# Reordering a few matmuls in the weight-loading chunk, and issuing two late stores from GpSimd

## The chip, the cores and the metric

The kernel runs on one core of one Trainium2 chip. The metric is the device time of one execution in microseconds (us), taken from several executions. The profile of one execution gives a trace of every instruction. The span in a trace, from the first to the last instruction, is 1.9 to 2.2 us shorter than the time of the same run, so traces can be compared by their spans.

The engines are PE (matmuls), ACT (ScalarE), DVE (VectorE), POOL (GpSimd) and SP (the sync engine, which mostly issues DMAs).

## The reference

Linear attention over 8 batches and 8 heads (sequence 576, head size 64), and then one MLP over all 4608 rows:

```python
q_s = softmax(q, axis=-1)          # written out with exp, max and sum
k_s = softmax(k, axis=2)
kv  = einsum('bhsd,bhse->bhde', k_s, v)
x   = einsum('bhsd,bhde->bhse', q_s, kv)      # -> 4608 x 512
h   = x @ w_in                     # 512 -> 2048
g   = h * (1.0 / (1.0 + exp(-beta * h)))
return g @ w_out                   # 2048 -> 512, float32
```

## The kernel before

The rows are worked off in 9 chunks of 512 rows: the first 512 rows of each batch, and one last chunk with the 64-row tails of all eight. A chunk has 16 MLP units. Unit `u` is a first product `h_u` (`mm_a`, 4 matmuls of 128x512), a tanh `th_u` on ACT, a combination `g_u` on DVE, and a second product into `acc_0` to `acc_3` (`mm_b`, 4 matmuls). The second product runs two units behind the first (`LAG = 2`). The order of each engine's instructions is fixed by hand, by the order in which the program names them; in the timelines below the engines' work comes in that order.

Chunk 0 is special. It runs while the weights are still being loaded: `w_in` comes in four blocks of 512 columns and `w_out` in four blocks of rows, each cast from float32 to bfloat16, most of them by GpSimd, in two halves. Units 12 to 15 need block 3 of `w_in`. Beside it the attention part of batch 1 is prepared: exponentials of q on ACT (`q_exp`), their sums and the multiplication by the inverse sums on DVE (`q_sum`, `q_mul`, the tile is `eq_485`), transposes on PE (`q_pet`, tiles `tp_0` to `tp_3`) with copies to `qsT`, eight exponentials of k on ACT (`kz_exp`, tile `ek`), and then the products `kv_0` and `kv_1`, from which chunk 1 gets its input.

```python
    tail_zero(0)
    pool_cast(("out", 1), ("in", 2), ("out", 2))
    tail_zero(1)
    pool_cast(("in", 3), ("out", 3))          # GpSimd's own order

    for u in range(4, NJ):
        mm_a(0, u)
        mm_b(0, u - LAG)
        if u in (9, 10):
            q_exp(1, u - 9)
        if u in (9, 11):
            q_sum(1, (u - 9) // 2)
        if u in (10, 12):
            q_mul(1, (u - 10) // 2)
        if u in (11, 13):
            for j in (u - 11, u - 10):
                q_pet(1, j, nc.scalar if u == 11 else nc.vector)
        if u >= 12:
            kz_exp(1, u - 12)
        if u == 14:
            vz_cast(1, 0, nc.vector, m=2)
    mm_b(0, NJ - 2)
    # ... kv_mm(1, 0), kv_mm(1, 1), last mm_b, x_mm(1, 0..3), then chunk 1
```

So PE's order around unit 12 is: `h_11`, second product of unit 9, transposes `tp_0` and `tp_1`, `h_12`, second product of unit 10.

The second part concerns the end of the kernel, the last stores of the last chunk:

```python
    def store(c, st):
        ...
        if c == B:
            lo, hi = ((0, 2), (0, 2), (2, 3), (3, 4))[st]
            ...
            evac(eng, o[:, st, :], acc[st][:])          # ACT for even st, DVE for odd
            if st == hi - 1:
                for e in range(2):
                    (nc.scalar if st == 2 or (st == 3 and e) else nc.sync).dma_start(...)
```

The two stores of `o_2` (128 KB each) and one half of `o_3` are issued by the scalar engine, the rest by sync.

The softmax here doesn't subtract the row's maximum and nothing guards it: scores larger than these inputs give would overflow.

Of the kernel before, what the change touches and what calls it, by code (L numbers as in the profile page):

```python
# [17 lines left out]
def kernel(  # L18
# [23 lines left out]
    NW = 2  # L42
    D1 = D + 1
    LAG = 2
    NCH = B + 1

    const = ctx.enter_context(tc.tile_pool(name="const", bufs=1))
    stage = ctx.enter_context(tc.tile_pool(name="stage", bufs=1))
# [203 lines left out]
    def kv_mm(b, jj, n=2, tag="att"):  # L252
        t = ps.tile([P, n, 2 * D1], F32, tag=tag, bufs=2 if tag == "att" else 1, name=f"kv{b}_{jj}")
        att_of[b, jj] = t
        for jl in range(n):
            j = n * jj + jl
            if b < NW:
                for i in range(RW):
                    nc.tensor.matmul(
                        t[:, jl, 0:D1],  # L260
                        ek[b][:, j, i, :],
                        va[b][:, j, i, :],
                        start=(i == 0),
                        stop=(i == RW - 1),
                    )
                continue
            for i in range(R):
                nc.tensor.matmul(
                    t[:, jl, :],
                    ek[b][:, i, 2 * j : 2 * j + 2, :].rearrange("p h d -> p (h d)"),  # L270
                    va[b][:, i, 2 * j : 2 * j + 2, :].rearrange("p h d -> p (h d)"),
                    start=(i == 0),
                    stop=False,
                )
            nc.tensor.matmul(
                t[:, jl, :],
                ekt[(b // 2) % 2][:, ds(j * P, P)],
                vt[(b // 2) % 2][:, b % 2, 2 * j : 2 * j + 2, :].rearrange("p h d -> p (h d)"),
                start=False,
                stop=True,  # L280
            )

    def kv_norm(b, jj, n=2):
        t = att_of.pop((b, jj))
        rk = work.tile([P, n, 1], F32, tag="rk", bufs=2, name=f"rk{b}_{jj}")
        nc.vector.reciprocal(rk[:], t[:, :, D : D + 1])
        for e in range(2):
            r = slice(e * D, (e + 1) * D)
            dst = kvp[r, b, n * jj : n * jj + n, e * D : (e + 1) * D]
            src = t[r, :, 0:D] if b < NW else t[r, :, e * D1 : e * D1 + D]  # L290
            nc.vector.tensor_tensor(dst, src, rk[r].to_broadcast((D, n, D)), ALU.mult)  # L291

    def x_mm(c, j, eng, tag="att"):
# [62 lines left out]
    def store(c, st):  # L356
        acc = acc_of[c]
        eng = nc.scalar if st % 2 == 0 else nc.vector
        if c == B:
            lo, hi = ((0, 2), (0, 2), (2, 3), (3, 4))[st]  # L360
            if st == lo:
                o_of[c] = stage.tile([P, R, DM], F32, tag="wo", bufs=4, name=f"o{c}_{lo}")
            o = o_of[c]
            evac(eng, o[:, st, :], acc[st][:])
            if st == hi - 1:
                for e in range(2):
                    (nc.scalar if st == 2 or (st == 3 and e) else nc.sync).dma_start(
                        out_t[:, MAIN:S, :].rearrange("(i e) t f -> e t i f", e=2)[e, :, lo:hi, :],
                        o[e * TAIL : (e + 1) * TAIL, lo:hi, :],
                    )  # L370
            return
        if st == 0:
            o_of[c] = stage.tile([P, R, DM], F32, tag="wo", bufs=4, name=f"o{c}")
        o = o_of[c]
        evac(eng, o[:, st, :], acc[st][:])
        if st % 2 == 1:
            ov = out[c * S : c * S + MAIN, :].rearrange("(p i) f -> p i f", i=R)
            nc.sync.dma_start(ov[:, st - 1 : st + 1, :], o[:, st - 1 : st + 1, :])
# [41 lines left out]
    ek_buf(1, nc.gpsimd)  # L420
    v_buf(1)

    def load_next(nb):
        if nb < B:
            load_q(nb)
            load_kv(k_st, k, nb, "k_st")
            load_kv(v_st, v, nb, "v_st")
        elif nb == B:
            load_qtail()

    def finish_b(c, j):
        mm_b(c, j)
        if j == NJ - 1:
            for st in range(R):
                store(c, st)
# [47 lines left out]
    w_cast("in", 1, 1, nc.vector)  # L483
    mm_b(0, 0)
    mm_b(0, 1)
    def pool_cast(*what):
        for kind, blk in what:
            for half in range(2):
                w_cast(kind, blk, half, nc.gpsimd)
# [10 lines left out]
    pool_cast(("in", 3), ("out", 3))  # L500

    for u in range(4, NJ):
        mm_a(0, u)
        mm_b(0, u - LAG)
        if u in (9, 10):
            q_exp(1, u - 9)
        if u in (9, 11):
            q_sum(1, (u - 9) // 2)
        if u in (10, 12):
            q_mul(1, (u - 10) // 2)  # L510
        if u in (11, 13):
            for j in (u - 11, u - 10):
                q_pet(1, j, nc.scalar if u == 11 else nc.vector)
        if u >= 12:
# [3 lines that stand above are left out]
# [17 lines left out]
    mm_b(1, 0)  # L535
    mm_b(1, 1)

    def side(c, u):
        b = c + 1
        if b > B:  # L540
            return
        tail = b == B
        o = 2 if c == 1 else 0
        if u in (2 + o, 3 + o):
            q_exp(b, u - 2 - o)
            q_sum(b, u - 2 - o)
        if u in (4 + o, 5 + o):
            q_mul(b, u - 4 - o)
            if not tail:
                k_exp(b, u - 4 - o)  # L550
        if u == 4 + o and not tail:
            v_buf(b)
            v_cast(b, nc.gpsimd)
            vtail_cast(b, nc.gpsimd)
        if u == 6 + o:
            if not tail:
                ktail_exp(b)
            q_xbar(b)
        if u in (8 + o, 10 + o) and not tail:
            kv_mm(b, (u - 8 - o) // 2)  # L560
            kv_norm(b, (u - 8 - o) // 2)
        if 11 <= u < 15:
            j = u - 11
            x_mm(b, j, nc.scalar if j % 2 == 0 else nc.vector)
        if u == 9:
            load_next(c + 2)

    for u in range(4):
        side(1, u)
    for c in range(1, NCH):  # L570
        for j in range(4 if c == 1 else 0, NJ - 1 if c == B else NJ):
            lead = c > 1 and j == 3
            if not lead:
                mm_a(c, j)
            if c > 1 and j == 2:
                mm_a(c, 3)
            if (c, j) == (B, NJ - 2):
                pass
            elif j >= LAG:
                mm_b(c, j - LAG)  # L580
            else:
                finish_b(c - 1, NJ + j - LAG)
            side(c, j)
    mm_a(B, NJ - 1, tag="att")
    last = [(0, j) for j in range(NJ - 4, NJ - 1)] + [(1, j) for j in range(NJ - 4, NJ - 1)]
    last += [(0, NJ - 1), (1, NJ - 1)] + [(st, j) for st in (2, 3) for j in range(NJ - 4, NJ)]
    for st, j in last:
        mm_b(B, j, [st])
        if j == NJ - 1:
            store(B, st)  # L590
# [1 line left out]
_INS = ['q', 'k', 'v', 'moe_w_in', 'moe_w_out', 'moe_beta']  # L592
_OUTS = [((4608, 512), 'float32')]
# [25 lines left out]
```

## Time and profile before

| what | value |
|---|---|
| time, median of 3 runs | 293.87 us (293.31 to 294.41) |
| profiled run: time, span, granted clock | 294.54 us, 292.4 us, 0.996 |
| PE busy | 279.5 us, 96% |
| PE idle before `acc_0` of unit 2 | 0.86 us |
| PE idle before `tp_0` | 1.59 us |
| end of the last copy (`o_3`) to the end of the span | 5.36 us |

From the page of the kernel before: its span, its part 1 (busy time of each engine with its share of the span and instruction count) and the engines' shares of part 4, the chain of waits that ended last.

```profile
span 292.4 us, 3879 instructions
PE 279.5 (96%) x1447; PEld 131.0 (45%) x1475; DVE 184.2 (63%) x299; ACT 163.9 (56%) x238; POOL 42.0 (14%) x55
PE 85%; DMA 6%; DVE 2%; ACT 1%; issue 1%; SPq 1%; another core or an unknown queue 1%; POOL 0%; ACTq 0%
```

PE is the bottleneck. From about 49 us to the last products it has no gaps worth naming, so only its gaps in chunk 0 and the tail after its last matmul can be won.

The timeline of the kernel before, in chunk 0. The columns are start in us, duration in us, engine, source line, operation, output and inputs, their shapes, the count; in square brackets the idle time of the engine just before, and what ended it.

```profile
22.15 1.37 POOL L140 CAST w_out_b<-w_out_100 128x1024 bf16<-128x1024 f32 x1 [4.28 <-DMA w_out_100<-in_moe_w_out_dram]
23.57 0.38 PE L344 MATMUL acc_0_377<-w_out_b,g_2_365 128*128 128x512 bf16 x1 [0.86 <-POOL w_out_b L140]
...
36.01 3.01 POOL L140 CAST w_in_b<-w_in_114 128x1024 bf16<-128x1024 f32 x2 [2.12 <-DMA w_in_114<-in_moe_w_in_dram]
36.04 2.09 DVE L226 TENSOR_TENSOR eq_485<-eq_485,rq_487 128x1024 bf16<-128x1024 bf16 x1
38.27 0.39 PE L245 MATMUL tp_0_521<-identity,eq_485 128*128 128x128 bf16 x4 [1.59 <-DVE eq_485 L226]
38.71 1.03 PE L316 MATMUL h_12_533<-xT_80,w_in_b 128*128 128x512 bf16 x4
39.78 0.69 ACT L326 ACTIVATE th_12_538<-h_12_533,beta_t 128x512 bf16<-128x512 f32 x1
```

Two gaps of PE: 0.86 us at 23.57, behind a GpSimd cast of `w_out` block 0, and 1.59 us at 38.27, behind the DVE multiply `eq_485`. GpSimd's cast of `w_in` block 3 (two halves, 36.01 to 39.02) starts before that multiply, when its DMA (landed at 35.89) has come in.

The timeline of the kernel before, at the end (SPq and ACTq are DMA issues on the sync and the scalar engine), and the DMA view of the same stores (the last column is the median time from issue to landing, in us).

```profile
286.06 1.31 ACTq L367 DMA_DIRECT2D out_dram<-o_2_2904  x2
286.31 0.69 DVE L140 COPY o_3_2912<-acc_3_2730 128x512 f32<-128x512 f32 x1 [1.03 <-PE acc_3_2730 L344]
287.03 0.95 SPq L367 DMA_DIRECT2D out_dram<-o_3_2912  x1
287.47 1.76 ACTq L367 DMA_DIRECT2D out_dram<-o_3_2912  x1
```

```profile
out_dram<-o_2_2904 ACTq DMA_DIRECT2D x2, 128.0 KB, 3.8
out_dram<-o_3_2912 SPq DMA_DIRECT2D x1, 128.0 KB, 4.2
out_dram<-o_3_2912 ACTq DMA_DIRECT2D x1, 128.0 KB, 4.0
```

The copy of `o_3` ends at 287.00. Sync issues its half at once, but the scalar queue is still issuing the stores of `o_2` and gets to its half only at 287.47.

### The profile page before, as it was taken

The page shows a single profiled execution, that of the slowest core. Times are in us where ns is not written, and L with a number is a line of the kernel's source. Part 1 is how long each engine was busy: PE and PEld are TensorE (multiplying, and loading weights), DVE is VectorE, ACT ScalarE, POOL GpSimd, SP SyncE. Part 2 cuts the span into 40 slices and gives each one's busy share as a digit, 9 for nine tenths or more (in the row PEclk, how much of TensorE's full clock was granted, in tenths as well). Part 3 has the DMA queues.
Part 4 walks back from the last instruction along what each step waited for, and adds up shares of the span by engine and source line. Part 5 has one row for each costly group of instructions (what it writes and reads, how often), then busy time and mean ns, then how long its engine had stood idle before and what let it go on. Part 6 is the DMA issues. An engine that isn't in the chain of part 4 may idle for free.

```text
span 292.4 us, 3879 instructions
## 1 busy us (share of the span) xinstructions
PE 279.5 (96%) x1447; PEld 131.0 (45%) x1475; DVE 184.2 (63%) x299; ACT 163.9 (56%) x238; POOL 42.0 (14%) x55
## 2 busy tenths in 40 slices
PE   8898979999999999999999999999999999999991
PEld 3443435445444444454445444544454444544440
DVE  7853696695578557855695469456954694563441
ACT  4863666684486448734773567346825654453340
POOL 4539670300030021002100110003000000000000
PEclk9999999999999999999999999999999999999998
DMA  7999999708932963297319821981293023012005
GB/s 243 378 385 371 377 385 311 248 2 233 296 152 62 315 162 123 62 326 177 123 40 302 223 90 54 303 234 64 84 165 52 32 115 72 0 58 87 0 0 144
DMA packets 55971, 50.06 MB, mean 171 GB/s; under 512 B 26241, under 2 KB 47761, under 8 KB 55953
## 3 DMA queue, kind: packets, MB, share of 16 engines
q1 hardware_dynamic: 55712, 49.43, 55.8%
q10 hardware_dynamic: 240, 0.39, 0.5%
q8 instruction: 11, 0.18, 0.3%
q14 instruction: 8, 0.06, 0.1%
HBM read 36.71 MB, written 9.44 MB: 158 GB/s over the span
## 4 chain that ended last, share of the span: by engine, by line
PE 85%; DMA 6%; DVE 2%; ACT 1%; issue 1%; SPq 1%; another core or an unknown queue 1%; POOL 0%; ACTq 0%
DMA w_out_100<-in_moe_w_out_dram 4%; DMA v_st_91<-in_v_dram 2%; PE acc_3_724 L344 1%; PE acc_2_2458 L344 1%; PE acc_0_2456 L344 1%; PE acc_3_2459 L344 1%; PE acc_1_2167 L344 1%; PE acc_1_1300 L344 1%; PE acc_1_1589 L344 1%; PE acc_1_2728 L344 1%; PE acc_1_1011 L344 1%; PE acc_1_722 L344 1%; PE acc_1_1878 L344 1%; PE acc_2_1879 L344 1%; PE acc_2_1590 L344 1%; PE acc_0_721 L344 1%
## 5 line engine op out<-in xcount | busy, mean ns | idle before, releaser
L316 PEld LDWEIGHTS <-w_in_b 128*128 128x128 bf16 x576 | 55.3, 98 | 65.5 <-issue 2.7
L386 PEld LDWEIGHTS <-kvp 128*128 128x128 bf16 x34 | 3.7, 117 | 6.2 <-issue 3.6
L140 POOL CAST va_2202<-v_st_2007 128x2048 bf16<-128x2048 f32 x1 | 1.9, 1919 | 29.5 <-DMA v_st_2007<-in_v_dram 29.5
L140 POOL CAST va_1913<-v_st_1718 128x2048 bf16<-128x2048 f32 x1 | 1.9, 1918 | 26.7 <-DMA v_st_1718<-in_v_dram 26.7
L140 POOL CAST va_1624<-v_st_1429 128x2048 bf16<-128x2048 f32 x1 | 1.9, 1922 | 26.6 <-DMA v_st_1429<-in_v_dram 26.6
L153 ACT ACTIVATE ek_144<-k_st_86 64x576 bf16<-64x576 f32 x8 | 5.5, 681 | 0.2
L153 ACT ACTIVATE ek_149<-k_st_118 64x576 bf16<-64x576 f32 x8 | 5.4, 676 | 0.0
L140 POOL CAST va_1046<-v_st_836 128x2048 bf16<-128x2048 f32 x1 | 1.9, 1920 | 24.0 <-DMA v_st_836<-in_v_dram 24.0
L140 POOL CAST va_1335<-v_st_1140 128x2048 bf16<-128x2048 f32 x1 | 1.9, 1917 | 22.7 <-DMA v_st_1140<-in_v_dram 22.7
L296 PEld LDWEIGHTS <-kvp 128*128 128x128 bf16 x32 | 3.1, 98 | 4.2 <-DVE kvp L291 1.0
L140 POOL CAST va_147<-v_st_91 128x576 bf16<-128x576 f32 x4 | 3.3, 860 | 6.3 <-DMA v_st_91<-in_v_dram 6.3
L209 ACT ACTIVATE eq_189<-q_st_83 128x1024 bf16<-128x1024 f32 x2 | 2.1, 1056 | 3.0 <-DMA q_st_83<-in_q_dram 3.0
L140 POOL CAST va_783<-v_st_132 128x2048 bf16<-128x2048 f32 x1 | 1.9, 1916 | 12.2 <-DMA v_st_132<-in_v_dram 12.2
L140 POOL CAST w_in_b<-w_in_114 128x1024 bf16<-128x1024 f32 x2 | 3.0, 1536 | 2.1 <-DMA w_in_114<-in_moe_w_in_dram 2.1
L226 DVE TENSOR_TENSOR eq_485<-eq_485,rq_487 128x1024 bf16<-128x1024 bf16 x2 | 3.3, 1652 | 0.0
L140 POOL CAST w_out_b<-w_out_100 128x1024 bf16<-128x1024 f32 x2 | 2.4, 1205 | 4.6 <-DMA w_out_100<-in_moe_w_out_dram 4.6
L140 POOL CAST w_out_b<-w_out_116 128x1024 bf16<-128x1024 f32 x2 | 2.6, 1292 | 1.7 <-DMA w_out_116<-in_moe_w_out_dram 1.7
L220 DVE TENSOR_REDUCE rq_191<-eq_189 128x16 f32<-128x1024 bf16 x2 | 2.4, 1215 | 0.3 <-ACT eq_189 L209 0.3
L220 DVE TENSOR_REDUCE rq_487<-eq_485 128x16 f32<-128x1024 bf16 x2 | 2.4, 1212 | 0.3 <-ACT eq_485 L209 0.3
L220 DVE TENSOR_REDUCE rq_748<-eq_746 128x16 f32<-128x1024 bf16 x2 | 2.4, 1212 | 0.3 <-ACT eq_746 L209 0.3
L220 DVE TENSOR_REDUCE rq_1887<-eq_1885 128x16 f32<-128x1024 bf16 x2 | 2.4, 1191 | 0.3 <-ACT eq_1885 L209 0.3
L220 DVE TENSOR_REDUCE rq_2176<-eq_2174 128x16 f32<-128x1024 bf16 x2 | 2.4, 1190 | 0.3 <-ACT eq_2174 L209 0.3
(1461 smaller groups left out, 838.9 us busy)
## 6 DMA issues: line engine op xcount, KB each, us to landing
k_st_86<-in_k_dram SPq DMA_DIRECT2D x4, 288.0 KB, 5.7
v_st_91<-in_v_dram SPq DMA_DIRECT2D x4, 288.0 KB, 6.5
k_st_118<-in_k_dram SPq DMA_DIRECT2D x4, 288.0 KB, 9.6
v_st_124<-in_v_dram SPq DMA_DIRECT2D x2, 576.0 KB, 9.3
q_st_83<-in_q_dram SPq DMA_DIRECT2D x2, 512.0 KB, 4.3
w_in_97<-in_moe_w_in_dram SPq DMA_DIRECT2D x2, 512.0 KB, 6.4
w_out_100<-in_moe_w_out_dram SPq DMA_DIRECT2D x2, 512.0 KB, 9.3
w_in_102<-in_moe_w_in_dram SPq DMA_DIRECT2D x1, 1024.0 KB, 9.3
```

Source lines behind the costliest of these rows:

```text
L140: eng.tensor_copy(dst, src)
L153: nc.scalar.activation(ek[b][r, j : j + m, :, e * D : (e + 1) * D], k_st[b][r, j : j + m, :].rearrange("p j (i d) -> p j i d", i=RW), ACTF ...
L209: nc.scalar.activation(eq[b][:, :, s * m : (s + 1) * m, :].rearrange("p i h d -> p h i d"), q_st[b][:, s * m : (s + 1) * m, :].rearrange(" ...
L220: nc.vector.tensor_reduce(rq[b][:, 0, :, h], eq[b][:, :, h, :], axis=AX.X, op=ALU.add)
L226: nc.vector.tensor_tensor(eq[b][:, :, h, :], eq[b][:, :, h, :], rq[b][:, 1, :, h].unsqueeze(3).to_broadcast((P, R, m, D)), ALU.mult,)
L296: nc.tensor.matmul(t[:], kvp[:, c, j, :], qsT[c][:, :, j, :])
L316: nc.tensor.matmul(h[:], w_in_b[:, kt, ds(j * P, P)], x_of(c)[:, kt, :], start=(kt == 0), stop=(kt == KT - 1),)
L344: nc.tensor.matmul(acc[st][:], g[:, ds(st * P, P)], w_out_b[:, j, :], start=(j == 0), stop=(j == NJ - 1),)
L386: nc.tensor.matmul(t[:, 0:cols], kvp[:, B - 1, 0, :], kvp[:, B - 1, :, :].rearrange("p j r -> p (j r)")[:, 0:cols],)
```

## The change

The intent has three parts. `h_5` goes ahead of unit 2's second product, so that PE has work in the gap at 23.57. `h_12` goes ahead of `tp_0` and `tp_1` (and `h_14` ahead of `tp_2` and `tp_3`), so that PE has work in the gap at 38.27. The two stores of `o_2` go to GpSimd, so that the scalar engine is free to issue its half of `o_3` when the copy ends. The core of the diff (the rest of it belongs to switches that are off, and does not change the instructions):

```diff
+    FIX, LASTMAIN, COLT = True, False, False
 ...
                 for e in range(2):
-                    (nc.scalar if st == 2 or (st == 3 and e) else nc.sync).dma_start(
+                    if FIX:
+                        q_eng = (nc.sync, nc.sync, nc.gpsimd, nc.scalar if e else nc.sync)[st]
+                    else:
+                        q_eng = nc.scalar if st == 2 or (st == 3 and e) else nc.sync
+                    q_eng.dma_start(
 ...
     for u in range(4, NJ):
-        mm_a(0, u)
+        if not (FIX and u == 5):
+            mm_a(0, u)
+        if FIX and u == 4:
+            mm_a(0, 5)
+            mm_b(0, 2)
+            continue
+        if FIX and u in (12, 14):
+            for j in (u - 12, u - 11):
+                q_pet(1, j, nc.scalar if u == 12 else nc.vector)
         mm_b(0, u - LAG)
 ...
-        if u in (11, 13):
+        if not FIX and u in (11, 13):
             for j in (u - 11, u - 10):
                 q_pet(1, j, nc.scalar if u == 11 else nc.vector)
```

In the order that the program names for ACT, `th_12` also goes ahead of the two `qsT` copies.

More of the change, by code (lines that the diff above doesn't have):

```diff
@@ L44 @@
     LAG = 2
+    FIX, LASTMAIN, COLT = True, False, False
     NCH = B + 1
+    order = list(range(NCH))
+    if LASTMAIN:
+        order[B - 1], order[B] = B, B - 1
+    LASTC = order[-1]
     const = ctx.enter_context(tc.tile_pool(name="const", bufs=1))
@@ L266, in kv_mm @@
                 continue
+            if COLT:
+                for i in range(R + 1):
+                    for e in range(2):
+                        hd = 2 * j + e
+                        nc.tensor.matmul(
+                            t[e * D : (e + 1) * D, jl, 0:D1],
+                            ek[b][:, i, hd, :] if i < R else ekt[(b // 2) % 2][:, ds(hd * D, D)],
+                            va[b][:, i, hd, :] if i < R else vt[(b // 2) % 2][:, b % 2, hd, :],
+                            start=(i == 0),
+                            stop=(i == R),
+                            tile_position=(0, e * D),
+                        )
+                continue
             for i in range(R):
@@ L289, in kv_norm @@
             dst = kvp[r, b, n * jj : n * jj + n, e * D : (e + 1) * D]
-            src = t[r, :, 0:D] if b < NW else t[r, :, e * D1 : e * D1 + D]
+            src = t[r, :, 0:D] if b < NW or COLT else t[r, :, e * D1 : e * D1 + D]
             nc.vector.tensor_tensor(dst, src, rk[r].to_broadcast((D, n, D)), ALU.mult)
@@ L358, in store @@
         eng = nc.scalar if st % 2 == 0 else nc.vector
+        if c == B and c != LASTC:
+            if st == 0:
+                o_of[c] = stage.tile([P, R, DM], F32, tag="wo", bufs=4, name=f"o{c}")
+            o = o_of[c]
+            evac(eng, o[:, st, :], acc[st][:])
+            if st % 2 == 1:
+                for e in range(2):
+                    nc.sync.dma_start(
+                        out_t[:, MAIN:S, :].rearrange("(i e) t f -> e t i f", e=2)[e, :, st - 1 : st + 1, :],
+                        o[e * TAIL : (e + 1) * TAIL, st - 1 : st + 1, :],
+                    )
+            return
         if c == B:
@@ L370, in store @@
                     )
+            return
+        if c == LASTC:
+            o = stage.tile([P, R, DM], F32, tag="wo", bufs=4, name=f"o{c}_{st}")
+            evac(eng, o[:, st, :], acc[st][:])
+            ov = out[c * S : c * S + MAIN, :].rearrange("(p i) f -> p i f", i=R)
+            (nc.sync, nc.scalar, nc.sync, nc.sync)[st].dma_start(ov[:, st, :], o[:, st, :])
             return
@@ L421, with load_next @@
     v_buf(1)
-    def load_next(nb):
-        if nb < B:
-            load_q(nb)
-            load_kv(k_st, k, nb, "k_st")
-            load_kv(v_st, v, nb, "v_st")
-        elif nb == B:
+    def load_next(n):
+        if order[n] < B:
+            load_q(order[n])
+        else:
             load_qtail()
+        if n < B:
+            load_kv(k_st, k, n, "k_st")
+            load_kv(v_st, v, n, "v_st")
     def finish_b(c, j):
@@ L502 @@
     for u in range(4, NJ):
-        mm_a(0, u)
+        if not (FIX and u == 5):
[3 more added lines that the diff above has]
+            mm_b(0, 2)
+            continue
+        if FIX and u in (12, 14):
+            for j in (u - 12, u - 11):
+                q_pet(1, j, nc.scalar if u == 12 else nc.vector)
         mm_b(0, u - LAG)
@@ L536, with side @@
     mm_b(1, 1)
-    def side(c, u):
-        b = c + 1
-        if b > B:
+    def side(n, u):
+        if n + 1 >= NCH:
             return
-        tail = b == B
-        o = 2 if c == 1 else 0
+        qc = order[n + 1]
+        kb = n + 1
+        o = 2 if n == 1 else 0
         if u in (2 + o, 3 + o):
-            q_exp(b, u - 2 - o)
-            q_sum(b, u - 2 - o)
+            q_exp(qc, u - 2 - o)
+            q_sum(qc, u - 2 - o)
         if u in (4 + o, 5 + o):
-            q_mul(b, u - 4 - o)
-            if not tail:
-                k_exp(b, u - 4 - o)
-        if u == 4 + o and not tail:
-            v_buf(b)
-            v_cast(b, nc.gpsimd)
-            vtail_cast(b, nc.gpsimd)
-        if u == 6 + o:
-            if not tail:
-                ktail_exp(b)
-            q_xbar(b)
-        if u in (8 + o, 10 + o) and not tail:
-            kv_mm(b, (u - 8 - o) // 2)
-            kv_norm(b, (u - 8 - o) // 2)
+            q_mul(qc, u - 4 - o)
+            if kb < B:
+                k_exp(kb, u - 4 - o)
+        if u == 4 + o and kb < B:
+            v_buf(kb)
+            v_cast(kb, nc.gpsimd)
+            vtail_cast(kb, nc.gpsimd)
+        if u == 6 + o:
+            if kb < B:
+                ktail_exp(kb)
+            q_xbar(qc)
+        if u in (8 + o, 10 + o) and kb < B:
+            kv_mm(kb, (u - 8 - o) // 2)
+            kv_norm(kb, (u - 8 - o) // 2)
         if 11 <= u < 15:
             j = u - 11
-            x_mm(b, j, nc.scalar if j % 2 == 0 else nc.vector)
-        if u == 9:
-            load_next(c + 2)
+            x_mm(qc, j, nc.scalar if j % 2 == 0 else nc.vector)
+        if u == 9 and n + 2 < NCH:
+            load_next(n + 2)
     for u in range(4):
         side(1, u)
-    for c in range(1, NCH):
-        for j in range(4 if c == 1 else 0, NJ - 1 if c == B else NJ):
-            lead = c > 1 and j == 3
-            if not lead:
+    for n in range(1, NCH):
+        c = order[n]
+        for j in range(4 if n == 1 else 0, NJ - 1 if n == B else NJ):
+            if not (n > 1 and j == 3):
                 mm_a(c, j)
-            if c > 1 and j == 2:
+            if n > 1 and j == 2:
                 mm_a(c, 3)
-            if (c, j) == (B, NJ - 2):
+            if (n, j) == (B, NJ - 2):
                 pass
@@ L581 @@
             else:
-                finish_b(c - 1, NJ + j - LAG)
-            side(c, j)
-    mm_a(B, NJ - 1, tag="att")
+                finish_b(order[n - 1], NJ + j - LAG)
+            side(n, j)
+    mm_a(LASTC, NJ - 1, tag="att")
     last = [(0, j) for j in range(NJ - 4, NJ - 1)] + [(1, j) for j in range(NJ - 4, NJ - 1)]
@@ L587 @@
     for st, j in last:
-        mm_b(B, j, [st])
+        mm_b(LASTC, j, [st])
         if j == NJ - 1:
-            store(B, st)
+            store(LASTC, st)
 _INS = ['q', 'k', 'v', 'moe_w_in', 'moe_w_out', 'moe_beta']
```

## The prediction

> **What bounds the kernel now.** The matmul engine: the page's first part has PE busy 279.5 of 292.4 us (96%); in the chain of waits PE has 85% of the span. From 49 us on that chain is an unbroken row of PE work (per MLP unit 0.86 us for each of its two products). The change leaves that part alone: the built instruction orders differ only in chunk 0 and in the last stores. So only PE's gaps in chunk 0 (18 to 51 us) and the tail after 284 us can pay.
>
> **Gaps in the timeline of before.**
> 1. acc_0 of unit 2 starts at 23.57 after 0.86 us idle: the second half of w_out block 0 (landed 22.1) is cast by GpSimd until 23.52.
> 2. Transposes tp_0/tp_1 start at 38.27 after 1.59 us idle, for the DVE multiply eq_485 (36.04 to 38.13; its twin takes 1.22, so I estimate 0.87 us of it as waiting for GpSimd's w_in cast beside it).
> 3. In the tail the scalar queue issues both stores of o_2 (286.06 to 287.37), then its half of o_3 from 287.47; the sync queue starts the other half at 287.03.
>
> **What the change does.** h_5 (0.86) goes into gap 1: units from h_6 on start about 0.8 us earlier. h_12 (0.86) goes before tp_0/tp_1, into gap 2. The gains do not add: PE now finishes acc of unit 9 near 35.7, but h_12 needs w_in block 3, whose cast starts at 36.0 when its DMA lands and ends at 37.0, and tp_0 needs eq_485. The DMA does not come earlier. I expect h_12 at 37.0 to 37.6, transposes at 38.0 to 38.5, acc of unit 10 at 38.7 to 39.0 instead of 39.58.
>
> Afterwards ScalarE limits: from 38.7 to 47.9 it is nearly full (per unit 0.58 tanh spacing + 1.39 for two ek exponentials, against PE's 1.73). th_12 now starts before the two qsT copies, at 38 to 38.5, so the last ek exponential ends at 47.0 to 47.6 instead of 47.9. DVE's last va cast (until 48.03) moves with th_15. So kv_1 (48.24) moves by 0.3 to 0.9; I take 0.6. Later chunks inherit it.
>
> Tail: with o_2's two 128 KB stores on GpSimd, the scalar queue's half of o_3 can start at 287.05 instead of 287.47. It landed last (287.47 + 4.0 = 291.5; sync's half 291.2), so 0.3 us at most. The GpSimd stores start near 286.1 and have 5 us to land unnoticed; scalar's took 3.8. The Trainium skill ("DMA: Bandwidth & Descriptors", Specifications) gives GpSimd-issued DMAs a first byte of about 1 us against 0.6; no run here shows that yet. I count -0.1 us on average, as a slow first GpSimd DMA could cost something.
>
> **Sum.** 293.87 - 0.6 - 0.1 = 293.2 us; range 292.3 to 294.3 (before's three runs span 1.1). Within 2%: 0.98; faster or slower by over 2%: 0.01 each.
>
> **What would show it.** Right: no idle before acc_0 of unit 2 beyond 0.2 us, h_6 near 25.3; a new PE wait of about 1.3 us before h_12 on GpSimd's w_in cast; ACT without gaps from th_12 to the last ek exponential; kv_1 at 47.3 to 48.0; unchanged spacing from there to the end; last DMA issue at 287.05 less the shift. Wrong: kv_1 not moved, or a last event that is a GpSimd store.
>
> **What would make it wrong.** GpSimd stores needing over 5 us; the earlier multiply colliding with GpSimd's casts and delaying h_12; loads shifting into other stores; noise larger than the effect.

## The result, and the profile after

| | before | after |
|---|---|---|
| time, median of 6 runs | 294.14 us (293.31 to 294.73) | 294.59 us (294.07 to 295.37) |
| ratio after/before, 95% interval | | 1.0023 (0.9998 to 1.0047) |
| profiled run: time, span, clock | 294.54, 292.4, 0.996 | 294.07, 291.9, 0.993 |

Executions over 1.5% slower than the fastest of the same kernel are left out of the means. A ratio here and below is the mean time of one kernel's fast runs over that of the other's of the same rounds, so it is not quite the ratio of the medians quoted beside it. The time lies above the predicted range of 292.3 to 294.3, and the sign of the difference is against the prediction.

The two profiled runs say the opposite: the changed kernel's is 0.47 us shorter than the other's. That is the first thing to explain. The page of the kernel after, its span and part 1:

```profile
span 291.9 us, 3879 instructions
PE 278.4 (95%) x1447; PEld 130.7 (45%) x1475; DVE 184.8 (63%) x299; ACT 163.7 (56%) x238; POOL 42.2 (14%) x57
```

The timeline of the kernel after, in chunk 0:

```profile
22.10 1.04 POOL L145 CAST w_out_b<-w_out_100 128x1024 bf16<-128x1024 f32 x1 [2.98 <-DMA w_out_100<-in_moe_w_out_dram]
24.66 0.38 PE L362 MATMUL acc_0_377<-w_out_b,g_2_365 128*128 128x512 bf16 x1
...
36.01 3.01 POOL L145 CAST w_in_b<-w_in_114 128x1024 bf16<-128x1024 f32 x2 [2.14 <-DMA w_in_114<-in_moe_w_in_dram]
36.26 1.87 DVE L231 TENSOR_TENSOR eq_485<-eq_485,rq_487 128x1024 bf16<-128x1024 bf16 x1
37.11 1.04 PE L334 MATMUL h_12_520<-xT_80,w_in_b 128*128 128x512 bf16 x4 [0.20 <-POOL w_in_b L145]
38.18 0.69 ACT L344 ACTIVATE th_12_525<-h_12_520,beta_t 128x512 bf16<-128x512 f32 x1 [1.41 <-PE h_12_520 L334]
38.27 0.38 PE L250 MATMUL tp_0_530<-identity,eq_485 128*128 128x128 bf16 x4
```

Both gaps are gone from where they were. `h_12` now fills the time before `tp_0`, which starts at 38.27 as before, `th_12` starts 1.60 us earlier (38.18 instead of 39.78), and the copy of `o_3` at the end starts 0.94 us earlier (285.37 instead of 286.31). So in this pair of traces the reordering is worth more than predicted. (This execution also began late: `h_4` started at 22.93 instead of 21.68, which the wait for the `w_in` block absorbed.)

The tail of the kernel after, timeline and DMA view:

```profile
285.37 0.69 DVE L145 COPY o_3_2912<-acc_3_2730 128x512 f32<-128x512 f32 x1 [1.03 <-PE acc_3_2730 L362]
285.40 1.18 POOL L401 DMA_DIRECT2D out_dram<-o_2_2904  x2 [85.55 <-ACT o_2_2904 L143]
286.09 0.50 SPq L401 DMA_DIRECT2D out_dram<-o_3_2912  x1
286.10 0.55 ACTq L401 DMA_DIRECT2D out_dram<-o_3_2912  x1
```

```profile
out_dram<-o_2_2904 POOLq DMA_DIRECT2D x2, 128.0 KB, 3.9
out_dram<-o_3_2912 SPq DMA_DIRECT2D x1, 128.0 KB, 4.6
out_dram<-o_3_2912 ACTq DMA_DIRECT2D x1, 128.0 KB, 4.8
```

The scalar half of `o_3` is indeed issued 0.04 us after the end of the copy (286.06) instead of 0.47. Yet the span ends 5.85 us after that copy, against 5.36 before: both halves of `o_3` need longer to land, 4.8 and 4.6 us instead of 4.0 and 4.2.

### The profile page after: what moved, and what is told of

The parts are those of the page before. It is cut to its first block, busy times and chain, and to the rows that moved or that the text cites. A ratio compares the mean times of both kernels' runs of the same rounds, so it can differ in the third digit from the quotient of the medians.

```text
span 291.9 us, 3879 instructions
## 1 busy us (share of the span) xinstructions
PE 278.4 (95%) x1447; PEld 130.7 (45%) x1475; DVE 184.8 (63%) x299; ACT 163.7 (56%) x238; POOL 42.2 (14%) x57
## 4 chain that ended last, share of the span: by engine, by line
PE 84%; DMA 8%; DVE 2%; POOL 1%; issue 1%; ACT 1%; SPq 0%; POOLq 0%
DMA w_in_114<-in_moe_w_in_dram 4%; DMA k_st_86<-in_k_dram 2%; DMA w_in_97<-in_moe_w_in_dram 2%; PE acc_0_2456 L362 1%; PE acc_3_724 L362 1%; PE acc_2_2458 L362 1%; PE acc_2_2729 L362 1%; PE acc_3_2459 L362 1%; PE acc_1_2728 L362 1%; PE acc_1_2167 L362 1%; PE acc_1_1300 L362 1%; PE acc_1_1011 L362 1%; PE acc_2_1879 L362 1%; PE acc_1_1589 L362 1%; PE acc_0_1588 L362 1%; PE acc_2_1301 L362 1%
## 5 line engine op out<-in xcount | busy, mean ns | idle before, releaser
L401 POOL DMA_DIRECT2D out_dram<-o_2_2904 x2 | 1.2, 590 | 85.6 <-ACT o_2_2904 L143 85.6
L145 POOL CAST va_147<-v_st_91 128x576 bf16<-128x576 f32 x4 | 2.7, 668 | 7.8 <-DMA v_st_91<-in_v_dram 7.5
L334 PE MATMUL h_0_316<-xT_80,w_in_b 128*128 128x512 bf16 x4 | 1.5, 380 | 1.5 <-POOL w_in_b L145 1.3
L145 DVE CAST w_in_b<-w_in_102 128x1024 bf16<-128x1024 f32 x2 | 2.6, 1314 | 0.0
L225 DVE TENSOR_REDUCE rq_748<-eq_746 128x16 f32<-128x1024 bf16 x2 | 2.4, 1214 | 0.3 <-ACT eq_746 L214 0.3
L225 DVE TENSOR_REDUCE rq_487<-eq_485 128x16 f32<-128x1024 bf16 x2 | 2.4, 1212 | 0.3 <-ACT eq_485 L214 0.3
L145 POOL CAST w_out_b<-w_out_100 128x1024 bf16<-128x1024 f32 x2 | 2.1, 1040 | 3.3 <-DMA w_out_100<-in_moe_w_out_dram 3.3
L225 DVE TENSOR_REDUCE rq_1887<-eq_1885 128x16 f32<-128x1024 bf16 x2 | 2.4, 1193 | 0.3 <-ACT eq_1885 L214 0.3
```

Source lines behind the costliest of these rows:

```text
L145: eng.tensor_copy(dst, src)
L225: nc.vector.tensor_reduce(rq[b][:, 0, :, h], eq[b][:, :, h, :], axis=AX.X, op=ALU.add)
L334: nc.tensor.matmul(h[:], w_in_b[:, kt, ds(j * P, P)], x_of(c)[:, kt, :], start=(kt == 0), stop=(kt == KT - 1),)
L401: q_eng.dma_start(out_t[:, MAIN:S, :].rearrange("(i e) t f -> e t i f", e=2)[e, :, lo:hi, :], o[e * TAIL : (e + 1) * TAIL, lo:hi, :],)
```

## The experiments

Each kernel ran in 5 rounds, alternating with the kernel before on the same chip. The kernel before had these medians: 293.99 us (293.12 to 294.64, 11 runs) in e1 to e4, 293.61 us (293.18 to 294.45, 11 runs) in e5 to e8, 293.91 us (293.17 to 294.93, 11 runs) in e9 to e12. All results were correct, and all verdicts are "same" at 2%; the question is one of less than a microsecond. In the traces of the experiments the tile names have no numbers.

The theory after the first pair of traces was: the reordering gains about 0.9 us and the GpSimd stores cost about 0.5 us, so the two partly cancel. The first rival was that the trace of before was an unlucky execution and the reordering gains nothing on average, so that only the cost of the stores is left. The second submission tests what makes an execution lucky: the order in which DVE's multiply and GpSimd's cast of `w_in` block 3 come to run (theory D where the expectations use letters).

### e1: the reordering alone

```diff
-                    if FIX:
+                    if False:          # all late stores as before
```

> The chunk 0 part of the change alone; the last stores as before. Theory A (the reorder saves about 0.94 us on PE, as o_3's copy at 285.37 against 286.31 in the first two traces shows, and the GpSimd stores give it back): 0.7 to 1.0 us faster than before on the mean (ratio 0.9966 to 0.9976), tail after o_3's copy about 5.4 us as before. Rival B (the reorder's gain is only that of one lucky trace; the average run has no gain): ratio 0.999 to 1.001. Rival C (the reorder itself is slower in most runs through later loads): ratio above 1.001.

Measured: fast runs 293.88 to 294.56 us, ratio 1.0010 (0.9991 to 1.0029). The reordering alone gains nothing that can be seen; a gain of 0.9 us, a ratio of 0.997, is outside the interval. One of its six runs took 600.83 us, and that was the profiled one. It tells nothing of the change; its page shows what happened:

```profile
PE 586.1 (98%) x1447; PEld 205.6 (34%) x1475; DVE 189.1 (32%) x299; ACT 164.8 (28%) x238; POOL 41.2 (7%) x55
```

DVE, ACT and POOL took about the time that they took before (DVE 189.1 us against 184.2), but the matmuls doubled: the median distance between the starts of two matmuls in a row was 443 ns, against 216 ns in the trace of before. The Trainium skill, page "TensorE: Matmul & The Clock Gate", section "Wait — 56ns, not 53.3ns?", gives 426.7 ns for a cold and 215.7 ns for a warm array at this size. The warm figure agrees with this case to 1 ns. The 443 ns are near the cold figure, but here they lasted a whole execution under full load. The clock of 1.0 in its result says nothing: this trace holds no record of the granted clock at all, and 1.0 is what an empty record gives, while all the other traces have one that begins with the full clock at 4.5 to 7.2 us. A clock that stayed low throughout is therefore not excluded. Why is open.

### e2: the GpSimd stores alone

```diff
-        if not (FIX and u == 5):
+        if True:
-        if FIX and u == 4:
+        if False:
-        if FIX and u in (12, 14):
+        if False:
-        if not FIX and u in (11, 13):
+        if u in (11, 13):
```

> The GpSimd stores of o_2 alone; chunk 0 as before. Theory A: slower than before by 0.9 to 1.8 us (ratio 1.003 to 1.006), and in the trace the stretch from the end of o_3's copy to the end of the span is 5.8 us or more against 5.4, while everything up to that copy stands at the times of before. Rivals B and C: within 0.3 us of before.

Measured: median 294.54 us (294.31 to 295.62), ratio 1.0023 (1.0004 to 1.0043). The stores alone make the kernel slower, by about 0.7 us of ratio and with an interval that leaves out 1, though by less than the 1.003 to 1.006 expected. In its trace the span ends 5.83 us after the copy of `o_3`.

### e3 and e4: both kernels again, unedited

> The changed kernel once more, for a second trace and fresh rounds. Theory A: ratio 1.000 to 1.004 as measured first, o_3's copy about 0.9 us earlier than in before's traces with the tail longer. Rival B: o_3's copy at the time of before. If the start of the first exponential of k varies between traces (7.2 in the trace of before, 8.5 in that of after), it should vary here too.

> The kernel before against itself: the noise. All theories: ratio 1.000 within 0.0015. Its trace tells how much the start (first exponential of k, h_4's start at 21.68) varies from run to run and whether the first product of chunk 1 still comes at about 50.7.

Measured: e3 (the changed kernel) median 294.73 us (294.03 to 296.03), ratio 1.0025 (1.0002 to 1.0048), so the first result repeats. e4 (the kernel before) median 293.50 us (293.09 to 296.66; one run is 3 us above the others, unexplained), ratio 1.0001 (0.9963 to 1.0038).

What these two were for is their traces. The timeline of the second trace of the kernel before:

```profile
35.47 1.21 DVE L226 TENSOR_TENSOR eq<-eq,rq 128x1024 bf16<-128x1024 bf16 x1
35.83 2.73 POOL L140 CAST w_in_b<-w_in 128x1024 bf16<-128x1024 f32 x2 [2.13 <-DMA w_in<-in_moe_w_in_dram]
36.83 0.61 PE L245 MATMUL tp<-identity,eq 128*128 128x128 bf16 x8 [0.71 <-DVE eq L226]
37.64 1.04 PE L316 MATMUL h<-xT,w_in_b 128*128 128x512 bf16 x4 [0.20 <-POOL w_in_b L140]
```

And the second trace of the changed kernel:

```profile
35.54 1.21 DVE L231 TENSOR_TENSOR eq<-eq,rq 128x1024 bf16<-128x1024 bf16 x1
35.96 2.67 POOL L145 CAST w_in_b<-w_in 128x1024 bf16<-128x1024 f32 x2 [2.15 <-DMA w_in<-in_moe_w_in_dram]
37.71 1.04 PE L334 MATMUL h<-xT,w_in_b 128*128 128x512 bf16 x4 [1.52 <-POOL w_in_b L145]
38.58 0.61 PE L250 MATMUL tp<-identity,eq 128*128 128x128 bf16 x8
```

In both, the multiply began earlier than in the first traces, by 0.57 us (e4) and 0.72 us (e3), and ran ahead of the cast. It then takes 1.21 us instead of 2.09 or 1.87, and in place of that the first half of the cast takes 1.75 us (e4) and 1.69 us (e3) instead of 1.04. The one that comes second waits for the first. The Trainium skill, page "SBUF — State Buffer", section "Summary: rules for kernel authors", says of a DVE operation with two inputs in SBUF, as the multiply has, and a GpSimd operation that reads SBUF that the second one to issue "fully blocks" until the first has finished; these durations agree, with either of the two as the blocked one.

Who comes first is a matter of some tenths of a microsecond: in the traces of kernels in which the order was left free, the multiply starts between 35.25 and 36.26 us and the load of block 3 lands between 35.51 and 36.44. The effect has opposite signs in the two kernels. In the old order PE has the transposes first, which need the multiply: an early multiply is good (`tp_0` at 36.83 instead of 38.27), and a late one holds up everything. In the new order PE has `h_12` first, which needs the cast: a late multiply costs nothing, but an early one delays `h_12` to 37.71, with the transposes behind it although their data has been there since 36.75.

### e5 to e8: forcing either order in either kernel

A one-column copy forces the order without breaking any dependence. For "cast first", DVE reads a column of the cast block before its multiply; for "multiply first", GpSimd reads an element of the multiply's result before it casts. e5 and e6 do this in the old order, e7 and e8 in the new one; the stores are the old ones in all four.

```diff
 # e5, e7: cast first
+        if u == 10:
+            nc.vector.tensor_copy(tick[:, 0:1], w_in_b[:, 0, 1536:1537])
         if u in (10, 12):
             q_mul(1, (u - 10) // 2)
 # e6, e8: multiply first
-    pool_cast(("in", 3), ("out", 3))
 ...
         if u in (10, 12):
             q_mul(1, (u - 10) // 2)
+        if u == 10:
+            nc.gpsimd.tensor_copy(tick[:, 1:2], eq[1][:, 0, 0, 0:1])
+            pool_cast(("in", 3), ("out", 3))
```

> Instruction order of before, with a one-column DVE copy that makes the DVE multiply of batch 1 wait for GpSimd's cast of w_in block 3 (cast first, always). Theory D: the two exclude each other, and who comes first is a race that the traces so far show falling both ways; cast first is the bad outcome for before's order (kv_0's reciprocal 12.1 us after the w_in load landed, against 11.2 with the multiply first). Expected: that distance 12.1 to 12.4, time 294.4 to 294.8, ratio to before 1.002 to 1.003, and less spread between runs. Rival B (chunk 0's order and race do not matter, only noise): ratio 1.000 within 0.001.

> Instruction order of before, with a one-column GpSimd copy that makes GpSimd's cast of w_in block 3 wait for the DVE multiply (multiply first, always). Theory D: the good outcome for before's order: kv_0's reciprocal 11.1 to 11.3 us after the w_in load landed if the multiply starts near 35.5, up to 11.6 if it starts at 36.0; time 293.2 to 293.6, ratio to before 0.998 to 0.9995. Rival B: ratio 1.000 within 0.001 and equal to e5_before_castfirst.

> The changed order of chunk 0 with the old last stores, cast first. Theory D: the good outcome for the changed order, h_12 at about 37.1 fills the wait: kv_0's reciprocal 11.1 to 11.4 us after the w_in load landed, time 293.3 to 293.7, 0.8 to 1.2 us faster than e5_before_castfirst but no faster than e6_before_multfirst. Rival B: like before.

> The changed order of chunk 0 with the old last stores, multiply first. Theory D: the bad outcome for the changed order: h_12 waits at the head of PE's queue until about 37.7 with the transposes, which could have run at 36.8, behind it, and th_12 comes before the qsT copies on ScalarE: distance 11.7 to 12.0, time 293.9 to 294.3, 0.5 to 0.8 us slower than e6_before_multfirst. Rival B: like before.

| | cast first | multiply first |
|---|---|---|
| old order | e5: 296.17 us (295.79 to 297.46), ratio 1.0089 (1.0068 to 1.0110) | e6: 294.35 us (293.78 to 297.60), ratio 1.0039 (1.0001 to 1.0077) |
| new order | e7: 294.22 us (294.02 to 294.96), ratio 1.0019 (1.0003 to 1.0035) | e8: 294.99 us (294.42 to 296.45), ratio 1.0047 (1.0025 to 1.0070) |

By the medians the sign of the reordering flips, as the race says: it is worth -1.95 us where the cast is forced first (no run of e7 is as slow as the fastest of e5), and +0.64 us where the multiply is forced first. The second figure is not clear of noise: the runs of e6 and e8 overlap, and their means differ by 0.38 us. The sizes are not those of a free-running kernel, because the forcing has a cost of its own: all four are slower than the kernel before, and all four missed the expected times on the slow side. In e5 the timeline shows it:

```profile
37.13 0.16 DVE L511 COPY tick<-w_in_b 128x1 bf16<-128x1 bf16 x1 [0.81 <-POOL w_in_b L141]
37.21 1.95 DVE L227 TENSOR_TENSOR eq<-eq,rq 128x1024 bf16<-128x1024 bf16 x1
39.31 0.61 PE L246 MATMUL tp<-identity,eq 128*128 128x128 bf16 x8 [2.42 <-DVE eq L227]
```

The multiply, made to wait for the first half of the cast, then lost to the second half as well, and PE stood idle for 2.42 us. At 40.05, 0.74 us after it had resumed, its clock fell. The window view of e5 (stretch, its length, then busy us and count of PE, PEld, DVE, ACT and POOL, then PEclk, DMA share, GB/s) shows it:

```profile
36.00:42.00 6.00, 3.58 (x19) 1.46 (x17) 4.33 (x6) 2.36 (x5) 4.27 (x4) 0.84 1.06 391
42.00:48.00 6.00, 5.95 (x31) 2.87 (x31) 4.06 (x7) 4.86 (x9) 0.96 (x2) 0.88 1.09 355
```

In both stretches the granted clock of before is 1.00. The records show half the clock for 3.41 us, with matmuls about 0.43 us apart. From 39.75 to 43.81 eleven distances between matmuls took 4.06 us, against 2.38 us at 216 ns each. So up to 1.69 of the 1.95 us can be the clock's. e6 and e8 begin the cast only about 0.3 us after the multiply has ended, and in e7 the multiply, like that of e5, begins after the first half of the cast and takes 1.95 us. These four therefore agree with the race in sign but do not prove it by themselves; the traces whose order was left free, in the table further down, are the better evidence.

### e9 and e10: the two halves of the reordering

```diff
 # e9: only h_5 early
-        mm_a(0, u)
+        if u != 5:
+            mm_a(0, u)
+        if u == 4:
+            mm_a(0, 5)
 # e10: only the transposes later
         mm_a(0, u)
+        if u in (12, 14):
+            for j in (u - 12, u - 11):
+                q_pet(1, j, nc.scalar if u == 12 else nc.vector)
         mm_b(0, u - LAG)
 ...                                # and the old call at u in (11, 13) taken out
```

> Only the move of h_5 ahead of unit 2's second product; transposes and stores as before. Theory D: PE and so the batch 1 exponentials run up to 0.8 us earlier when the start is early, so the multiply starts near 35.5 and wins the race against the w_in cast, the good outcome for before's place of the transposes: kv_0's reciprocal about 11.2 us after the w_in load landed, time 293.3 to 293.7, ratio to before 0.998 to 1.000. Rival B: 1.000. If both parts of the reorder were simply bad, it would be slower than before.

> Only the transposes one unit later; h_5 and stores as before. Theory D: the result follows the race: with the cast first kv_0's reciprocal 11.2 us after the w_in load landed, with the multiply first 11.8; mean time 293.6 to 294.3, ratio 0.999 to 1.002. Rival (transposes later are a plain gain, as predicted at first): ratio 0.997.

Measured: e9 median 293.33 us (293.11 to 294.11), ratio 0.9986 (0.9968 to 1.0003). e10 median 294.09 us (293.43 to 294.48), ratio 1.0009 (0.9990 to 1.0029). Neither interval leaves out 1. In the trace of e9 the multiply came first (35.25, duration 1.21 us, load landed at 35.51) and in that of e10 second (36.24, duration 1.98 us, load landed at 35.98). These are each the good case of their order. One would expect that an earlier `h_5` brings all later units forward, and with them the multiply, which is good for the old order of the transposes and bad for the new one, so that the two parts of the reordering work against each other. That is only an argument. With one trace each, how often each case occurs in each kernel was not counted, and the first trace of the changed kernel, with `h_5` early but a late begin, had a late multiply all the same.

### e11: the stores of o_2 on sync instead

```diff
-                    (nc.scalar if st == 2 or (st == 3 and e) else nc.sync).dma_start(
+                    (nc.scalar if st == 3 and e else nc.sync).dma_start(
```

> Before, with o_2's two stores on the sync queue instead of the scalar queue; no GpSimd store. This frees the scalar queue at o_3's copy end as the change did, without GpSimd. Theory T (the last landing is set by moving the 1 MB of the last four tiles and by when each queue's data starts, not by the issue of o_3's scalar half): the scalar half of o_3 is issued 0.03 us after the copy instead of 0.47, and the end of the span still comes 5.2 to 5.8 us after the copy (before 5.36, with GpSimd 5.83). Rival (issue slot sets it): 4.9 us.

Measured: median 294.41 us (293.36 to 294.61), ratio 1.0014 (0.9996 to 1.0032). The timeline of its tail:

```profile
284.14 3.91 SPq L367 DMA_DIRECT2D out_dram<-o  x5
285.11 0.69 DVE L140 COPY o<-acc 128x512 f32<-128x512 f32 x1 [1.04 <-PE acc L344]
285.84 0.56 ACTq L367 DMA_DIRECT2D out_dram<-o  x1
```

The scalar half of `o_3` is issued right after the copy here too, without any work on GpSimd, and the span ends 5.41 us after the copy, much as in the kernel before. The test is not a clean one, though: sync now issues five stores, and its half of `o_3` goes out only 1.51 us after the copy instead of 0.03. The last landing is then that half's, at 4.46 us after the copy, against 4.51 us before, when the last issue came at 0.47 us. So the last landing did not follow the time of the last issue, an early issue of the scalar half alone brought nothing, and the longer tail appears only with GpSimd's stores. The Trainium skill, page "DMA: Bandwidth & Descriptors", section "Issuing engines are not separate DMA queues", says that issuing from several engines saves only the sequencer time of the initiation; that agrees.

### e12: load and attention part swapped

If the landing of `w_in` block 3 and the race behind it set the pace, the cure is to take them apart: load block 3 before the q of batch 1, and do the attention part of batch 1 later.

```diff
-    load_q(1, parts=2)
     w_load("in", 3)
+    load_q(1, parts=2)
 ...
+    pool_cast(("in", 3))
     tail_zero(1)
-    pool_cast(("in", 3), ("out", 3))
+    pool_cast(("out", 3))
 ...                # h_5 early, as in e9
-        if u in (9, 10):
-            q_exp(1, u - 9)          # q_sum, q_mul, q_pet and kz_exp likewise
+        if u in (11, 12):            # one or two units later; vz_cast on GpSimd;
+            q_exp(1, u - 11)         # q_pet(1, 2) and q_pet(1, 3) around kv_mm
```

> A version meant to beat both: h_5 ahead, w_in block 3 loaded before q of batch 1, so that its cast has no race with the multiply and h_12 does not wait; q exponentials, sums, multiplies and transposes of batch 1 two units later; va casts of batch 1 on GpSimd; two of the transposes in place of the two warm-up matmuls; old last stores. Theory D (the wait for w_in block 3 and the race bound the end of chunk 0): w_in block 3 lands near 33, PE runs on without a wait over 0.3 us from h_6 to h_15, kv_0's reciprocal at 45.8 to 46.5 against 47.0 to 48.0, time 292.2 to 293.2, ratio 0.995 to 0.998. Rival B: no gain beyond noise. If ScalarE's exponentials alone bound the end of chunk 0: reciprocal at 47.

Measured: median 292.62 us (292.33 to 295.44), ratio 0.9974 (0.9943 to 1.0004). Five of its six runs, at 292.33 to 292.79, lie below all 11 runs of the kernel before; the sixth, 295.44, is unexplained and makes the interval wide, so a gain is likely but not proven at 95%. The timeline:

```profile
32.99 2.02 POOL L140 CAST w_in_b<-w_in 128x1024 bf16<-128x1024 f32 x2 [0.69 <-DMA w_in<-in_moe_w_in_dram]
36.23 1.03 PE L316 MATMUL h<-xT,w_in_b 128*128 128x512 bf16 x4
39.20 1.21 DVE L226 TENSOR_TENSOR eq<-eq,rq 128x1024 bf16<-128x1024 bf16 x1
45.58 0.38 PE L245 MATMUL tp<-identity,eq 128*128 128x128 bf16 x4 [0.96 <-DVE eq L226]
```

The cast is done four microseconds before the multiply begins, both run at their short durations, and `h_12` needs no wait. Two gaps are left: 0.68 us before `h_6`, at 25.87, where the expectation was no wait over 0.3 us, and one at 45.58: the second multiply now meets GpSimd's casts of v, and takes 1.89 us. This version beats both kernels in its median, and it still has the same conflict in another place. It changes several things at once (loads, `h_5`, attention part, casts of v, warm-up matmuls); which of them brings the gain was not tested, and e9, with `h_5` alone, was 0.6 us faster by the medians, within noise.

### All traces together

The times are those of each trace, in us from the start of the span. The distance is the end of the copy of `o_3` minus the landing of `w_in` block 3, which both were read from the traces (the landing from the DMA's semaphore record); the tail is the end of the span minus the end of that copy.

| trace | order on PE | block 3 landed | multiply start | first | distance | tail | span |
|---|---|---|---|---|---|---|---|
| before | old | 35.89 | 36.04 | cast | 251.11 | 5.36 | 292.36 |
| e4 (before again) | old | 35.71 | 35.47 | multiply | 250.23 | 5.38 | 291.32 |
| e2 (stores only) | old | 36.44 | 36.08 | multiply | 250.12 | 5.83 | 292.39 |
| e11 (stores on sync) | old | 35.60 | 35.34 | multiply | 250.21 | 5.41 | 291.21 |
| e9 (`h_5` only) | old transposes | 35.51 | 35.25 | multiply | 250.21 | 5.36 | 291.08 |
| after | new | 35.89 | 36.26 | cast | 250.17 | 5.85 | 291.91 |
| e3 (after again) | new | 35.84 | 35.54 | multiply | 250.82 | 5.80 | 292.46 |
| e10 (transposes only) | new transposes | 35.98 | 36.24 | cast | 250.16 | 5.36 | 291.50 |
| e5 (forced) | old | 35.94 | 37.21 | cast | 253.49 | 5.33 | 294.76 |
| e6 (forced) | old | 35.93 | 35.71 | multiply | 250.68 | 5.34 | 291.95 |
| e7 (forced) | new | 35.47 | 36.73 | cast | 251.08 | 5.33 | 291.87 |
| e8 (forced) | new | 35.74 | 35.46 | multiply | 251.26 | 5.33 | 292.34 |

In the eight free traces the distance is 250.12 to 250.23 us in six, whichever the order on PE. It is larger in the two whose race went the wrong way for their order: 251.11 in the first trace of the kernel before and 250.82 in the second trace of the changed one. Measured from the landing, the best case of both orders is thus the same to about 0.1 us. The losing case has one trace in each order, so this rests on few executions.

What sets the pace is not the same in both, however. In the four old-order traces with the multiply first, the copy ends 250.47 or 250.48 us after the start of the multiply, a closer tie than that to the landing. In the two new-order traces with the cast first it ends 250.16 and 250.17 us after the landing, but 249.80 and 249.90 us after the start of the multiply. So the old order's good case follows the multiply, and the new one's follows the landing and the cast. The multiply in turn starts 3.63 or 3.64 us after `th_9` in all eight, so it follows PE's pace, and here the first gap comes in: where PE waits 0.86 us before `acc_0` of unit 2, the multiply starts at 36.04 to 36.24 (before, e2, e10), and where it does not, in the old order, at 35.25 to 35.47 (e4, e9, e11). That gap, too, is an outcome of one execution: e4 and e11 have PE's old order and no such wait.

The forced kernels pay their own cost within the distance, and e12, whose block 3 landed at 32.93 and no longer sets the pace, is left out (tail 5.36, span 290.74).

## Why the prediction was wrong

**The step on chunk 0, which failed.** The prediction said: "So kv_1 (48.24) moves by 0.3 to 0.9; I take 0.6. Later chunks inherit it." In the trace after, `kv_1` did start at 47.28, 0.96 us earlier. But it rested on "tp_0/tp_1 start at 38.27 after 1.59 us idle, for the DVE multiply eq_485 (36.04 to 38.13; its twin takes 1.22, so I estimate 0.87 us of it as waiting for GpSimd's w_in cast beside it)". The mechanism and the 0.87 us were right (2.09 against 1.21 us). What failed was taking the order of these two, and with it the wait of 1.59 us, as a property of the kernel, when it was the outcome of one execution; the same holds of gap 1. In the kernel's other trace (e4) the multiply ran first, `tp_0` started at 36.83, and `kv_1` at 47.17, which is where the change brings it in its own good case. There `acc_0` of unit 2 did not wait either, and PE's waits before `tp_0` and `h_12` were 0.71 and 0.20 us. The free traces in the table give the same best distance from the landing for both orders. Measured over fast runs, the reordering is worth a ratio of 1.0010 (0.9991 to 1.0029) in place of the 0.998 that 0.6 us would give. The prediction even listed "the earlier multiply colliding with GpSimd's casts and delaying h_12" as a way to be wrong. This is what e3 shows, with `h_12` at 37.71 after 1.52 us of idle PE, and the transposes behind it.

**The tail, which failed in sign.** The prediction said "0.3 us at most" and counted "-0.1 us on average"; the step that failed is that the GpSimd stores "have 5 us to land unnoticed". They landed in time (3.9 us, median), but not unnoticed. The tail is 5.80 to 5.85 us in the three traces with GpSimd's stores and 5.33 to 5.41 us in the nine others of the table, a loss of 0.47 us between the means. That the scalar half of `o_3` would be issued right after the copy was right, but e11 shows no gain from it. The packet records show what the stores of `o_2` do: their first data packet comes 2.37 to 2.40 us after the issue from GpSimd (three traces), and 1.80 us after the issue from the scalar engine. In the first pair of traces, relative to the end of the `o_3` copy, that is +1.74 us instead of +0.87. Their packets then lie beside those of `o_3`, whose last half lands 4.78 to 4.82 us after the copy instead of 4.48 to 4.53 (4.46 in e11). From that last landing to the end of the span 1.03 us go by instead of 0.85 in the first pair, with three instead of one of the final waits of the sync engine left. In that pair the first difference is 0.31 us (4.82 against 4.51) and the second 0.18, together the 0.49 us by which its tails differ; that the overlapping packets cause the first of them is inferred from the records and was not tested by itself. Nor was it tested whether DVE's copy of `o_3`, which runs from 285.37 to 286.06 beside GpSimd's issues from 285.40 on, delays them. The prediction's warning from the Trainium skill (page "DMA: Bandwidth & Descriptors", section "Specifications": a first byte after about 1 us from GpSimd and about 0.6 us from sync and scalar) pointed the right way: the measured difference is 0.57 to 0.60 us, the page's is 0.4. It was noted but not carried into the sum.

**The sum.** Predicted was -0.7 us: -0.6 and -0.1. Measured was +0.45 us between the medians of the first result and +0.74 us in e3. With +0.47 us from the tail this leaves between -0.02 and +0.27 us for the reordering, which is zero within the spread of the runs. The two errors, about 0.6 us each, add up to the miss.

**What was right.** The gains of the two gaps do not add up. There is no idle time before `acc_0` of unit 2 in the trace after (but none in e4 either, without the change). `h_12` waits for GpSimd's cast of block 3 (37.11; predicted 37.0 to 37.6), though for 0.20 us by the timeline and not 1.3, since this execution began late. ACT is without gaps from `th_12` to the last exponential. The last store to land is not one of GpSimd's but the scalar half of `o_3`. The spacing of the later chunks is unchanged: `kv_1` moved by 0.96 us between the two traces and the copy of `o_3` by 0.94. "noise larger than the effect" was named, too; a single trace is one sample of that noise.

**What stays open.** How often either outcome of the race occurs in each kernel; whether e12's gain of about 1.3 us by the medians holds over more runs, and which of its edits brings it; the single runs of e4, e6 and e12 that are 2.6 to 3 us longer than all others of their kernel; and the one execution of e1 at half the matmul pace.

## What to carry to other kernels

When a trace shows a wait behind two operations that exclude each other, and they start within a few tenths of a microsecond of each other, look at a second trace of the same kernel before reordering anything: the wait may be the outcome of a race, and an order that is best for one outcome can be worst for the other. Take the rivals apart in time, as e12 does, rather than choosing which consumer goes first. Before moving the last stores to an idle engine, compare the time from issue to the first packet on both: the issue slot gained here was worth nothing, and the moved stores then overlapped with the last one.

## What the Trainium skill lacked or had wrong

- "DMA: Bandwidth & Descriptors", section "Specifications": the first-byte figures (about 1 us and 0.6 us) are well below the time from issue to the first data packet of the 128 KB stores here, 2.37 to 2.40 us from GpSimd and 1.80 us from scalar, both with packets of the `o_0` stores under way. The first of those, from sync and with no store under way, took 1.33 us. The page does not say that GpSimd's stores near the end lengthen a kernel's tail: 5.80 to 5.85 us against 5.33 to 5.41 us.
- "SBUF — State Buffer", section "Summary: rules for kernel authors": it has the blocking of whichever issues second, but not that the winner can change from one execution of the same kernel to the next (multiply 2.09 or 1.21 us, cast 1.04 or 1.75 us), nor that a kernel's distance from the landing to the last copy differed by 0.6 to 0.9 us between the two.
- "TensorE: Matmul & The Clock Gate", section "What's actually happening": it gives an idle window of about 3.4 us for the return to the cold state. In e5 an idle time of PE of only 2.42 us was followed by half the clock, 0.74 us after PE had resumed with 0.44 us of transposes; in e8 an idle time of 1.96 us was not. The length of the slow stretch, 3.41 us, is that of the page's window.
- The same page, section "Seeing it yourself", warns that clock records can be unreliable and knows of a clock stuck low for 50 us and more, but not of a whole execution under load at half the pace: e1's profiled run, with 443 ns between matmuls instead of 216 ns, and 600.83 us, in a trace that holds no record of the clock.
